# First four tiles as one group of four tokens, with scores by head pair

## The chip, the cores and the metric

The kernel runs on one core of a Trainium2 chip. The metric is the time of one execution in microseconds of device time; smaller is better. A core has five engines that each work through a queue of their own in order: TensorE (PE, matrix products), VectorE (DVE), ScalarE (ACT), GpSimd (POOL) and SyncE (SP, which here issues nearly all DMAs). PEld stands for TensorE's loads of the stationary operand. They meet only through semaphores.

## The reference

Attention over 4 batches, 8 heads, 768 positions and a head size of 64, with a window of 96 positions, 8 global positions at the start and a linear distance penalty, is followed by a feed-forward layer that takes the largest of three products.

```python
scores = q @ k.T / sqrt(64)
rel = pos[:, None] - pos[None, :]
is_global = pos[None, :] < 8
is_local  = (rel >= 0) & (rel < 96)
dist   = where(is_global & ~is_local, 96, abs(rel))
scores = scores - slope[h] * dist          # slope[h] = 2 ** -(h + 1)
scores = where(is_global | is_local, scores, -1e9)
a   = softmax(scores)
x   = (a @ v), heads side by side          # 3072 tokens x 512
h   = max(x @ w1, x @ w2, x @ w3)          # 512 x 768 each
out = h @ w_out                            # 768 x 512
```

## The kernel before, in words

A tile is 128 tokens; there are 24 tiles, six to a batch, and t is the tile's place in its batch. Everything is computed in bf16 with fp32 sums in PSUM. Since the window is 96 long, a tile of queries needs the keys of its own tile and of the one before it; the 8 global positions are put in place of the first 8 keys of the earlier tile, which no query of the window reaches (`put_kg`, `put_vg`; letters G and V).

The order of the work is written out in the string `SCHEDULE`. Each word is a unit: a letter, then the tile or chunk, then a choice of engine where there is one (0 ACT, 1 DVE, 2 POOL, and for transposes 4 stands for a DMA transpose on SP). Each engine's queue is the order in which the units name that engine. The units that matter here:

- `l`, `c`, `x`: load, cast to bf16 and transpose (PE, then a copy out of PSUM) of q and k for a group of tiles, listed in `GROUPS`. A group of n tiles gives each partition n neighbouring tokens, so one descriptor of the load reads n x 256 bytes, and the copy out of PSUM puts tokens back in their order. Before, tiles 0 to 11 come in groups of 2, 2, 2, 4 and 2.
- `L`, `C`, `X`: the same for single tiles 12 to 23; `v` loads a tile of v, and `C` with a 1 in its second place casts it.
- `K`: one exponential per head on ACT that makes the multiplicative mask `wmask` (line 300). `B`: one product per head that makes the additive mask `bias` (line 295).
- `S`: scores of one tile for four heads (two matmuls of 64 rows at a time, line 283), and one exponential out of PSUM on ACT into P (line 288). Where its last number is 1, a matmul of `bias` by the identity (line 275) puts the mask into PSUM ahead of the scores.
- `M`: the product of P and `wmask` on DVE (lines 307 and 309), left out where `bias` was used.
- `A`: 8 or 16 matmuls of P by v with a column of ones (lines 322 and 325), then on DVE the reciprocal of the sum and the product that gives `xb` (lines 331 and 332).
- `T`: transposes `xb` into `xT`, by PE and a copy (lines 349 and 350), or by DMA (line 340).
- `w`, `W`, `o`, `Q`: load and cast of the feed-forward weights. w1 to w3 come in two pieces each: columns 0 to 255 and the 512 columns behind them.
- `F c.f.j`: the product of chunk c with the 128 columns f of weight j, four matmuls (line 361). j = 0 is copied out of PSUM by ACT (line 366); j = 1 and 2 are taken into the running maximum by DVE (lines 368 and 370). A chunk is 4, 2, 2, 4, 4, 4 or 4 tiles (`sizes`). Three PSUM buffers (`psH`) serve all of them.
- `O`: the output product of one tile, six matmuls of 512 columns (line 376), a copy (line 382) and the store. `E`: the last chunk's outputs. `D`: dummy matmuls of zeros.

The string is a fixed order, so what an engine waits for is decided by it alone, and not by the order in which data arrive.

Of the kernel before, what the change touches and what calls it, by code (L numbers as in the profile page):

```python
# [25 lines left out]
    K0 K1 K2 K3 K4 K5 l1.0 l1.1 D0.3 c0.0.2 B0.1 B1.1 B2.1 B3.0 K6 B4.1 B5.1 c0.1.1 c1.0.2 x0.0.4 B6.1  # L26
    B7.1 x0.1.4 S0.0.1 v0 l2.0 l2.1 K7 S0.1.1 G0.0 S1.0.1 S1.1.0 x1.0.3 c1.1.2 M0.0 M0.1 M1.0 v1 x1.1.4
    C0.1.2 v2 A0.1 G1.2 S2.0.1 M1.1 c2.0.2 x2.0.1 C1.1.1 S2.1.0 G2.2 S3.0.1 M2.0 M2.1 C2.1.1 T0.1 S3.1.1
    M3.0 M3.1 c2.1.2 v3 A1.0 C3.1.0 w0.0 V1.2 x2.1.2 w1.0 A2.1 V2.2 A3.0 T1.0 T2.1 T3.1 W1.0.1 W0.0.0
    G3.2 S4.0.0 S4.1.0 F0.0.0 F0.1.0 M4.0 F0.2.0 F0.3.0 G4.1 S5.0.0 M4.1 S5.1.0 w0.1 W0.1.1 w0.2 W0.2.2  # L30
    V3.2 F0.0.1 F0.1.1 F0.0.2 F0.1.2 v4 C4.1.0 A4.0 V4.2 w1.1 W1.1.2 W2.0.0 F0.4.0 F0.5.0 M5.0 M5.1 w1.2
    W1.2.2 v5 W2.1.0 T4.0 F0.2.1 F0.3.1 l3.0 l3.2 F0.4.1 l3.1 c3.0.2 c3.2.2 F0.5.1 o2 C5.1.0 A5.1 l3.3
    F0.2.2 Q2.2 F0.3.2 W2.2.0 o0 T5.0 F0.4.2 o1 F0.5.2 x3.0.0 F1.0.0 F1.1.0 c3.1.1 F1.2.0 x3.2.0 Q0.2
    F1.0.1 F1.1.1 F1.2.1 l4.0 l4.1 c3.3.0 F1.0.2 F1.1.2 F1.2.2 x3.1.2 x3.3.1 F1.3.0 F1.4.0 Q1.2 F1.3.1
    S6.0.0 S6.1.0 v6 v7 v8 G6.0 F1.3.2 F1.5.0 v9 c4.0.1 F1.4.1 S7.0.0 S7.1.0 G7.2 v10 M6.0 M6.1 M7.0
    M7.1 O0.0.0 F1.4.2 c4.1.1 C6.1.2 C7.1.2 L12 F1.5.1 S8.0.0 S8.1.0 x4.0.0 O0.1.0 A6.0 x4.1.2 A7.1 V7.2
    F1.5.2 v11 T6.0 O0.2.0 T7.1 G8.2 C8.1.2 S9.0.0 S9.1.0 G9.1 v12 v13 O0.3.0 F2.0.0 F2.1.0 S10.0.0 M8.0
    M8.1 M9.0 M9.1 S10.1.0 C9.1.2 L13 L14 F2.0.1 F2.1.1 F2.0.2 A8.0 C12.0.1 F2.1.2 G10.2 O1.0.0 V8.2
    A9.1 X12.1 M10.0 M10.1 C10.1.0 C11.1.0 F2.2.0 S11.0.0 S11.1.0 M11.0 M11.1 L15 F2.3.0 F2.4.0 O1.1.0
    V9.2 A10.1 F2.2.1 V10.2 T8.0 F2.3.1 F2.5.0 T9.0 A11.1 F2.4.1 T10.0 F2.2.2 F2.3.2 T11.1 F2.4.2  # L40
    S12.0.0 S12.1.0 F2.5.1 C13.0.2 C14.0.2 C15.0.1 X13.4 F3.0.0 F3.1.0 F3.0.1 G12.1 C12.1.0 F3.2.0
    F3.1.1 F3.2.1 S13.0.0 S13.1.0 F2.5.2 v14 C13.1.0 C14.1.2 M12.0 M12.1 F3.0.2 F3.1.2 X14.4 F3.2.2
    X15.4 G13.2 M13.0 M13.1 S14.0.0 S14.1.0 F3.3.0 F3.4.0 F3.5.0 M14.0 M14.1 G14.1 A12.0 A13.1 F3.3.1
    F3.4.1 F3.5.1 S15.0.0 M15.0 S15.1.0 G15.0 v15 V13.2 L16 L17 v16 T12.4 v17 M15.1 O2.0.0 C15.1.0 A14.0
    V14.2 F3.3.2 F3.4.2 T13.4 F3.5.2 C16.1.0 C16.0.2 X16.3 T14.4 C17.0.2 A15.1 X17.4 O2.1.0 S16.0.0
    S16.1.0 G16.1 L18 V15.2 L19 T15.1 M16.0 O3.0.0 M16.1 F4.0.0 F4.1.0 F4.0.1 F4.1.1 C18.0.2 L20 C19.0.2
    A16.1 F4.2.0 F4.3.0 S17.0.0 S17.1.0 F4.2.1 F4.0.2 F4.3.1 v18 M17.0 v19 M17.1 X18.3 X19.4 C20.0.0
    V16.2 F4.1.2 C17.1.2 O3.1.1 A17.1 F4.2.2 F4.3.2 S18.0.0 M18.0 S18.1.0 M18.1 F4.4.0 T16.4 T17.4
    F4.4.1 C18.1.2 C19.1.1 F4.4.2 X20.4 G18.1 S19.0.0 S19.1.0 F4.5.0 L21 M19.0 M19.1 v20 F4.5.1 A18.0
    T18.4 F4.5.2 A19.1 T19.4 V19.1 C21.0.1 X21.4 G19.1 L22 C22.0.2 L23 X22.4 O3.2.1 O3.3.0 O4.0.1  # L50
    S20.0.0 S20.1.0 M20.0 G20.0 O4.1.0 F5.0.0 F5.1.0 F5.2.0 S21.0.0 S21.1.0 G21.2 F5.0.1 F5.1.1 M20.1
    M21.0 F5.3.0 F5.0.2 F5.1.2 F5.2.1 F5.2.2 v21 C20.1.1 C21.1.2 F5.4.0 S22.0.0 M21.1 S22.1.0 C23.0.0
    F5.3.1 M22.0 M22.1 F5.5.0 F5.3.2 A20.0 V20.2 G22.2 v22 F5.4.1 X23.4 v23 F5.5.1 T20.4 A21.1 V21.1
    T21.4 F5.4.2 F5.5.2 S23.0.0 S23.1.0 M23.0 O4.2.0 M23.1 C22.1.2 A22.0 C23.1.0 O4.3.0 V22.2 T22.4
    A23.1 T23.4 O5.0.1 O5.1.0 O5.2.1 O5.3.0 F6.0.0 F6.1.0 F6.0.1 F6.0.2 F6.2.0 F6.3.0 F6.4.0 F6.1.1
    F6.2.1 F6.1.2 F6.3.1 F6.4.1 F6.2.2 F6.3.2 F6.5.0 F6.4.2 F6.5.1 F6.5.2 E
# [4 lines left out]
def kernel(  # L61
# [27 lines left out]
    sizes = [4, 2, 2, 4, 4, 4, 4]  # L89

    GROUPS = [[0, 2], [2, 2], [4, 2], [6, 4], [10, 2]]
# [8 lines left out]
    NSTART = sizes[0]  # L100
# [21 lines left out]
    zeros = persist.tile([128, 512], BF16, name="zeros")  # L122
# [3 lines left out]
    bias = persist.tile([128, 2, 2, 2, 3, 128], BF16, name="bias")  # L126
    NVA = 4
    va_ring = [persist.tile([128, H * 65], BF16, name=f"va{i}") for i in range(NVA)]
    va_first = [persist.tile([128, H * 65], BF16, name=f"vaf{i}") for i in range(2)]
    kg8 = [persist.tile([128, NP, NG], BF16, name=f"kg8_{i}") for i in range(2)]  # L130
# [5 lines left out]
    va, masked = {}, {}  # L136
# [7 lines left out]
    def part(n, s):  # L144

        T0, sz = GROUPS[n]
        jn = {2: 4, 4: 2, 6: 1}[sz]
        a, x = divmod(s, 4 // jn)
        return divmod(T0, NT) + (sz, a, x * jn, jn)

    def load_part(n, s):

        bb, t0, sz, a, j0, jn = part(n, s)
        r = raw_pool.tile([128, 2 * DM], FP32, name="rawp", tag="raw")
        r = r[:, 0:sz * jn * 128].rearrange("i (h x) -> i h x", h=2 * jn)
        raw["p", n, s] = r
        src = (q, k)[a][bb, 2 * j0:2 * (j0 + jn), t0 * 128:(t0 + sz) * 128, :]
        nc.sync.dma_start(out=r, in_=src.rearrange("h (i e) d -> i h (e d)", e=sz))
# [19 lines left out]
    def cast_part(n, s, how):  # L178
        bb, t0, sz, a, j0, jn = part(n, s)
        qk = cast_pool.tile([128, 2 * DM], BF16, name="qkp", tag="qkb")  # L180
        qk = qk[:, 0:sz * jn * 128].rearrange("i (e h d) -> i e h d", e=sz, d=D)
        qb["p", n, s] = qk
        copies[how](qk, raw["p", n, s].rearrange("i h (e d) -> i e h d", e=sz))  # L183
# [42 lines left out]
    def u_x(n, s, how):  # L226
# [14 lines left out]
        for (lo, hi, pool, tag, copy), tp in zip(halves, tps):  # L241

            copy(dst[:, lo:hi], tp.rearrange("c e j i -> c j i e"))  # L243
# [24 lines left out]
    def u_S(T, g, how):  # L268
# [3 lines left out]
        if how:  # L272

            for hh in range(2):
                nc.tensor.matmul(sp[:, hh, :, 0:n], identb,  # L275
                                 bias[:, g, hh, :, 0:2] if t else bias[:, g, hh, :, 2:3],
                                 start=True, stop=False, skip_group_check=True)
        for ds in range(2 if t else 1):
            for j2 in range(2):
                jp = 2 * g + j2  # L280
                for hh in range(2):
                    hsl = slice(64 * hh, 64 * hh + 64)
                    nc.tensor.matmul(sp[:, hh, j2, ds], qT(T - ds, 1)[hsl, jp], qT(T, 0)[hsl, jp],  # L283
                                     start=not how, stop=True, skip_group_check=True)
        P = p_pool.tile([128, 4, 2, 128], BF16, name="P", tag="P")
        Pt[T, g] = P
        masked[T, g] = how
# [3 lines left out]
    def u_B(h, how):  # L291
        g, hp = divmod(h, 4)
        j2, hh = divmod(hp, 2)
        mul = (nc.scalar.mul, nc.vector.tensor_scalar_mul, nc.gpsimd.tensor_scalar_mul)[how]
        mul(bias[:, g, hh, j2], rbase, -slopes[h] / scale)
# [6 lines left out]
    def u_M(T, g):  # L302
        P = Pt[T, g]
        if masked[T, g]:
            return
        if T % NT:
            nc.vector.tensor_mul(P, P, wmask[:, g, :, 0:2])  # L307
        else:
            nc.vector.tensor_mul(P[:, :, 0], P[:, :, 0], wmask[:, g, :, 2])

    def u_A(T, how):

        b, t = divmod(T, NT)
        op = psS.tile([128, 2, 512], FP32, name="op", tag=f"sp{how}")
        for g in range(2):
            P = Pt[T, g]
            for j2 in range(2):
                for hh in range(2):
                    h = 4 * g + 2 * j2 + hh
                    i = 2 * hh + j2  # L320
# [189 lines left out]
```

The softmax here doesn't subtract the row's maximum and nothing guards it: scores larger than these inputs give would overflow.

## Time and profile before

| What | Value |
|---|---|
| median of 3 runs | 180.32 us (180.25 to 180.33) |
| span of the profiled execution | 178.5 us |
| what lies around that span, from the median | 1.8 us |
| granted TensorE clock, mean | 0.997 |
| PE busy | 167.1 us (94% of the span) |
| DVE, ACT, POOL busy | 119.1, 103.2, 37.4 us |
| first feed-forward matmul | 23.3 us |

The page gives no other time for the profiled execution than its span; the median of the runs is measured without the profiler's cut at the first and last instruction, and the difference is taken as constant. A row of the groups gives line, engine, operation, names and shapes, how often, then busy time, mean length of one in ns, and the engine's idle time just before such instructions with what ended it. Matmuls overlap, so the cost of one is read from the chain, where a stretch of so many matmuls has a length, and not from its mean length.

### The profile page before, as it was taken

What the parts mean: (1) busy time and instruction counts of PE and PEld (TensorE: products, weight loads), DVE (VectorE), ACT (ScalarE), POOL (GpSimd) and SP (SyncE); (2) the same over time, 40 slices, a digit from 0 to 9 for tenths busy, and PEclk for the clock granted to TensorE, in tenths of its full rate; (3) what the DMA queues carried; (4) which work ended last, traced back from release to release, by engine and by line L of the source; (5) the groups of instructions that cost most, each with busy time, mean ns of one, the idle gap of its engine ahead of it and who ended that gap; (6) DMA issues with size and microseconds to landing.
All of it is one profiled execution on the core that took longest, in us unless ns stands there. A gap on an engine that the chain in (4) does not pass through costs nothing.

```text
span 178.5 us, 3963 instructions
## 1 busy us (share of the span) xinstructions
PE 167.1 (94%) x1529; PEld 95.9 (54%) x1551; DVE 119.1 (67%) x237; ACT 103.2 (58%) x160; POOL 37.4 (21%) x65
## 2 busy tenths in 40 slices
PE   3599799999999999999999999999999999999991
PEld 0455645458866677845555555454454555444451
DVE  4519975977796689748978448978358986137610
ACT  4867898646689958555753936351862543440131
POOL 4255203543343012210006024100020401000000
PEclk9999999999999999999999999999999999999998
DMA  5999999999998899899544999988989664700015
GB/s 139 292 270 243 357 321 383 319 361 356 252 194 229 218 254 227 142 204 234 92 90 122 167 253 231 145 172 152 182 156 300 123 129 147 252 12 4 0 47 190
DMA packets 83587, 35.52 MB, mean 199 GB/s; under 512 B 66160, under 2 KB 78320, under 8 KB 83568
## 3 DMA queue, kind: packets, MB, share of 16 engines
q1 hardware_dynamic: 83424, 35.20, 83.6%
q8 instruction: 12, 0.20, 0.5%
q10 hardware_dynamic: 144, 0.07, 0.1%
q14 instruction: 7, 0.06, 0.1%
HBM read 25.17 MB, written 6.29 MB: 176 GB/s over the span
## 4 chain that ended last, share of the span: by engine, by line
PE 88%; ACT 3%; DVE 2%; POOL 2%; issue 1%; DMA 1%; POOLq 0%; ACTq 0%
PE h L361 53%; PE po L376 16%; PE sp L283 7%; PE op L322 3%; PE op L325 3%; PE tpp L239 3%; PE xtp L349 2%; ACT wmask L300 2%; PE sp L275 2%; DMA out_dram<-ost 1%; DVE qkT L243 1%; DVE xb L332 1%; ACT ost L382 1%; ACT P L288 1%; PE tp L261 1%
## 5 line engine op out<-in xcount | busy, mean ns | idle before, releaser
L361 PE MATMUL h<-xT,w 128*128 128x512 bf16 (+1 forms) x491 | 99.2, 348 | 0.7 <-issue 0.2
L361 PEld LDWEIGHTS <-w 128*128 128x128 bf16 x504 | 47.0, 98 | 40.4 <-ACT w L427 0.2
L288 ACT ACTIVATE P<-sp 128x1024 bf16<-128x1024 f32 (+1 forms) x48 | 43.4, 954 | 20.4 <-PE sp L283 20.2
L368 DVE TENSOR_TENSOR h<-h,h 128x512 bf16<-128x512 bf16 (+1 forms) x42 | 25.2, 609 | 25.6 <-PE h L361 15.5
L366 ACT CAST h<-h 128x512 bf16<-128x512 f32 (+1 forms) x42 | 21.6, 532 | 21.5 <-PE h L361 21.3
L376 PE MATMUL po<-wo,ht 128*128 128x512 bf16 (+2 forms) x147 | 33.1, 362 | 0.5
L370 DVE TENSOR_TENSOR ht<-h,h 128x512 bf16<-128x512 bf16 (+1 forms) x42 | 25.0, 606 | 3.7 <-PE h L361 3.0
L307 DVE TENSOR_TENSOR P<-P,wmask 128x1024 bf16<-128x1024 bf16 x36 | 24.8, 716 | 3.6 <-ACT P L288 3.5
L382 ACT COPY ost<-po 128x512 f32<-128x512 f32 (+2 forms) x20 | 11.2, 564 | 18.4 <-PE po L376 11.2
L376 PEld LDWEIGHTS <-ht 128*128 128x128 bf16 x156 | 14.0, 98 | 13.8
L332 DVE TENSOR_TENSOR xb<-op,rz 128x512 bf16<-128x512 f32 x24 | 16.6, 691 | 0.8
L283 PEld LDWEIGHTS <-qkT 64*128 64x128 bf16 x352 | 10.2, 96 | 10.0 <-issue 8.0
L283 PE MATMUL sp<-qkT 64*128 64x128 bf16 x352 | 15.2, 223 | 0.4 <-DVE xb L332 0.4
L322 PEld LDWEIGHTS <-P 128*128 128x128 bf16 x192 | 12.5, 97 | 2.7 <-ACT P L288 0.2
L221 POOL COPY va<-vaf 8x260 int32<-8x260 int32 x14 | 6.3, 449 | 34.7 <-PE op L325 34.7
L198 POOL CAST qkb<-raw 128x1024 bf16<-128x1024 f32 x7 | 7.2, 1037 | 27.6 <-DMA raw<-in_k_dram 27.6
L322 PE MATMUL op<-va,P 128*128 128x65 bf16 x160 | 12.4, 193 | 0.3 <-ACT va L189 0.2
L239 PE MATMUL tpp<-identb,qkp 128*128 128x128 bf16 x96 | 8.5, 246 | 4.0 <-POOL qkp L183 3.5
L325 PEld LDWEIGHTS <-P 128*128 128x128 bf16 x160 | 10.4, 97 | 1.8 <-issue 0.2
L239 PEld LDWEIGHTS <-qkp 128*128 128x128 bf16 x96 | 7.0, 112 | 5.8 <-POOL qkp L183 4.4
L325 PE MATMUL op<-va,P 128*128 128x65 bf16 x128 | 9.9, 193 | 0.1
L243 ACT COPY qkT<-tpp 128x1024 bf16<-128x1024 bf16 (+1 forms) x9 | 7.9, 873 | 3.4 <-PE tpp L239 3.4
(66 smaller groups left out, 107.7 us busy)
## 6 DMA issues: line engine op xcount, KB each, us to landing
rawv<-in_v_dram SPq DMA_DIRECT2D x24, 256.0 KB, 4.9
out_dram<-ost SPq DMA_DIRECT2D x23, 256.0 KB, 2.3
rawp<-in_q_dram SPq DMA_DIRECT2D x6, 512.0 KB, 7.3
rawp<-in_k_dram SPq DMA_DIRECT2D x6, 512.0 KB, 7.7
wst<-in_moe_w_dram SPq DMA_DIRECT2D x3, 1024.0 KB, 10.3
raw<-in_q_dram SPq DMA_DIRECT2D x12, 256.0 KB, 4.2
raw<-in_k_dram SPq DMA_DIRECT2D x12, 256.0 KB, 4.7
wst<-in_moe_w_dram SPq DMA_DIRECT2D x3, 512.0 KB, 8.6
```

Source lines behind the costliest of these rows:

```text
L239: nc.tensor.transpose(tp[:, e, j - lo], qb["p", n, s][:, e, 2 * j:2 * j + 2].rearrange("i h d -> i (h d)"), identb)
L283: nc.tensor.matmul(sp[:, hh, j2, ds], qT(T - ds, 1)[hsl, jp], qT(T, 0)[hsl, jp], start=not how, stop=True, skip_group_check=True)
L288: nc.scalar.activation(P[:, :, 0:n], sp.rearrange("p a b d n -> p (a b) d n")[:, :, 0:n], AF.Exp, bias=0.0, scale=scale)
L307: nc.vector.tensor_mul(P, P, wmask[:, g, :, 0:2])
L322: nc.tensor.matmul(o, P[:, i, 0], heads(va[T])[:, h], start=True, stop=(t == 0), skip_group_check=True)
L325: nc.tensor.matmul(o, P[:, i, 1], heads(va[T - 1])[:, h], start=False, stop=True, skip_group_check=True)
L332: nc.vector.tensor_tensor(out=x.rearrange("p (g h) d -> p g h d", g=2), in0=o4[:, :, :, 0:64], in1=rz[:, :, :, None].to_broadcast([128, 2, ...
L361: nc.tensor.matmul(ps, w123[f // 2][:, dm, j, (f % 2) * 128:(f % 2) * 128 + 128], xT[c][:, dm], start=(dm == 0), stop=(dm == 3))
L366: nc.scalar.copy(h01, ps)
L368: nc.vector.tensor_max(h01s[c, f], h01s[c, f], ps)
L370: nc.vector.tensor_max(ht[c][:, f], h01s[c, f], ps)
L376: nc.tensor.matmul(po, ht[c][:, f, tt * 128:(tt + 1) * 128], wo[:, f, cols], start=(f == 0), stop=(f == NF - 1))
```

## The change

The first four tiles become one group of four tokens in a partition, in eight pieces: q and k by head pair (64 x 2 columns). Queries of these tiles are copied out of PSUM as they stand, by token within the group and then by partition (`u_x`, for n = 0 and a = 0), and keys are put in order as before.

New units: `s tp.jp` computes the scores of one head pair for two tiles (tp = 0: tiles 0 and 1; tp = 1: tiles 2 and 3). The queries are read as four blocks of 32 columns. The exponential reads PSUM in the order of tokens and writes P in natural order, in two instructions of 384 elements for tp = 0 and one of 1024 for tp = 1. `m tp.jp` multiplies such a P by `wmask` on DVE or POOL. `g T.jp` puts the global keys in place of tile 1's first 8 keys (for tile 2's queries), and for tile 3's queries makes a copy `k2x` of tile 2's keys with the global ones in it, since tile 2's own keys are still needed. The three parts of `wmask` stand in another order. The unit `B`, the tensor `bias` and its matmuls are gone. P of tiles 2 and 3 is held in a buffer of the weight staging pool.

Chunks are now 2, 2, 2, 2, 4, 4, 4, 4 tiles, where two neighbours share `xT` and `ht`. `A` with a 2 uses two `psH` buffers and normalises in two halves. `load_w` can load in two halves. The dummy matmuls have 128 columns, and the order is a new one: tiles 8, 12 to 23 have `xb` transposed by DMA (before: 12, 13, 14, 16 to 23), and tiles 13 to 23 have q and k transposed by DMA (before: 13, 14, 15, 17, 19 to 23).

```diff
-    sizes = [4, 2, 2, 4, 4, 4, 4]
-    GROUPS = [[0, 2], [2, 2], [4, 2], [6, 4], [10, 2]]
+    sizes = [2, 2, 2, 2, 4, 4, 4, 4]
+    GROUPS = [[0, 4], [4, 2], [6, 4], [10, 2]]
...
+    BIG = [0, 0, 1, 1, 2, 3, 4, 5]
...
-        jn = {2: 4, 4: 2, 6: 1}[sz]
+        jn = 1 if n == 0 else {2: 4, 4: 2, 6: 1}[sz]
...
+            if n == 0 and a == 0:
+                copy(batch_T(0)[:, 0, j0 + lo:j0 + hi, 0:sz * 128].rearrange("c j (e i) -> c j e i", e=sz),
+                     tp.rearrange("c e j i -> c j e i"))
+            else:
+                copy(dst[:, lo:hi], tp.rearrange("c e j i -> c j i e"))
...
-        if how:
-
-            for hh in range(2):
-                nc.tensor.matmul(sp[:, hh, :, 0:n], identb,
-                                 bias[:, g, hh, :, 0:2] if t else bias[:, g, hh, :, 2:3],
-                                 start=True, stop=False, skip_group_check=True)
...
-        mul(bias[:, g, hh, j2], rbase, -slopes[h] / scale)
+    def u_g(T, jp, how):
+
+        k0 = qT(0, 1)[:, jp, 0:NG]
+        if T == 1:
+            copies[how](qT(1, 1)[:, jp, 0:NG], k0)
+        else:
+            copies[how](k2x[:, jp, NG:128], qT(2, 1)[:, jp, NG:128])
+            copies[how](k2x[:, jp, 0:NG], k0)
+
+    def u_s(tp, jp, how):
+
+        sp = psS.tile([128, 2, 4, 128], FP32, name="sp", tag=f"sp{how}")
+        g, j2 = divmod(jp, 2)
+        tiles = (2 * tp, 2 * tp + 1)
+        lo = 0 if tp else 1
+        for i, T in enumerate(tiles):
+            for ds in range(2 if T else 1):
+                for hh in range(2):
+                    hsl = slice(64 * hh, 64 * hh + 64)
+                    qs = qkT[0][hsl, 0, jp, 0:512].rearrange("c (e i) -> c e i", e=4)[:, :, 32 * T:32 * T + 32]
+                    ks = k2x[hsl, jp] if T - ds == 2 and ds else qT(T - ds, 1)[hsl, jp]
+                    nc.tensor.matmul(sp[:, hh, 2 * i + ds if T else 1], ks, qs,
+                                     start=True, stop=True, skip_group_check=True)
+        if tp:
+            if "P1" not in Pt:
+                Pt["P1"] = stage_pool.tile([128, 4, 2, 4, 128], BF16, name="P1", tag="wst1")
+            P = Pt["P1"][:, jp]
+        else:
+            P = p_pool.tile([128, 2, 4, 128], BF16, name="P0", tag="P")
+        Pt["s", tp, jp] = P
+        for hh in range(1 + lo):
+            o, x = (P[:, hh, 1:4], sp[:, hh, 1:4]) if lo else (P.rearrange("p h b n -> p (h b) n"),
+                                                               sp.rearrange("p h b n -> p (h b) n"))
+            nc.scalar.activation(o.rearrange("p b (i e) -> p b i e", e=4), x.rearrange("p b (e i) -> p b i e", e=4),
+                                 AF.Exp, bias=0.0, scale=scale)
+
+    def u_m(tp, jp, how):
+        g, j2 = divmod(jp, 2)
+        P = Pt["s", tp, jp]
+        mul = (nc.vector, nc.gpsimd)[how].tensor_mul
+        if tp:
+            wm = wmask[:, g, j2::2, 1:3].rearrange("p a s n -> p a (s n)")[:, :, None].to_broadcast([128, 2, 2, 256])
+            Pv = P.rearrange("p h (i s) n -> p h i (s n)", i=2)
+            mul(Pv, Pv, wm)
+        else:
+            mul(P[:, :, 1:4], P[:, :, 1:4], wmask[:, g, j2::2])
...
+        if how == 2:
+            ops = [psH.tile([128, 512], FP32, name="op", tag="h") for _ in range(2)]
```

The new order up to the first blocks of the feed-forward layer's second weight column:

```diff
+    K0 l0.6 K4 K2 c0.6.2 x0.6.1 K3 K5 l0.0 c0.0.2 x0.0.3 l0.4 c0.4.2 K1 x0.4.4 l0.2 c0.2.1 x0.2.3 l0.1
+    g2.0.1 K7 s0.0.1 c0.1.2 s0.2.0 l0.5 c0.5.1 x0.5.4 l0.3 l0.7 c0.7.1 x0.1.3 c0.3.2 g2.2.1 K6 g1.2.2
+    g1.0.2 g2.1.1 x0.3.2 x0.7.3 s0.1.1 s0.3.0 g1.1.2 s1.0.1 m0.2.0 s1.2.0 w0.0.0 g1.3.1 g2.3.1 s1.3.1 v0
+    C0.1.1 m0.3.0 m0.1.0 m0.0.0 A0.2 m1.0.0 s1.1.0 v1 C1.1.2 m1.3.0 W0.0.0 A1.1 m1.1.0 m1.2.1 D5.6 T0.0
+    V1.2 T1.1 v2 C2.1.2 A2.2 V2.0 F0.0.0 v3 C3.1.2 G0.0 A3.1 V3.0 w1.0.0 W2.0.2 w0.1.0 T2.0 F0.4.0
+    F0.1.0 T3.0 F0.5.0 W1.0.1 W0.1.2 F0.1.1 w0.2.0 W0.2.2 l1.0 c1.0.2 G3.0 F1.0.0 F1.0.1 F1.1.0 F1.1.1
+    F1.2.0 F0.1.2 F0.2.0 l1.1 c1.1.1 x1.0.2 F0.0.1 F0.0.2 x1.1.4 F1.1.2 F1.4.0 S4.0 S4.1 G4.2 F1.0.2
```

## The prediction, made before the changed kernel ran

> **What bounds the kernel now.** I read the page's slices first, then busy time by stage, what TensorE (PE) waited for, the chain of waits, and the groups by form for prices. The slices (4.46 us each) show an idle PE only at the start and in the last slice:
>
> ```profile
> PE   3599799999999999999999999999999999999991
> ```
>
> Cut into stages at the joints of the chain, per stage length, PE busy, weight load, DVE, ACT and POOL busy:
>
> ```profile
> 3.76:9.50 5.74, 2.84 (x23) 2.06 (x24) 3.88 (x10) 4.47 (x11) 1.84 (x2) 1.00 1.21 297
> 9.50:13.45 3.95, 3.95 (x37) 2.32 (x37) 0.19 (x1) 3.18 (x6) 2.06 (x4) 1.00 1.24 269
> 13.45:18.50 5.05, 4.67 (x67) 2.61 (x66) 5.02 (x8) 3.81 (x5) 2.24 (x3) 1.00 1.28 244
> 18.50:23.30 4.80, 3.84 (x85) 3.22 (x85) 4.11 (x11) 4.20 (x6) 0.94 (x3) 1.00 1.07 370
> 23.30:172.10 148.80, 147.59 (x1302) 83.63 (x1322) 104.18 (x195) 83.80 (x129) 28.14 (x42) 1.00 0.82 190
> ```
>
> From 23.30 to 172.10 PE is busy 147.59 of 148.80 us, and all that its waits hold after 23.3 is one line:
>
> ```profile
> PE h L361 <- issue: 0.2, 1, 0.2
> ```
>
> So the time is three terms: the start of the first feed-forward matmul (23.30), the PE work that is left then (148.8), and a tail of 6.4 us that the change leaves as it is. The chain (start, length, what) shows what sets the first, and PE's prices:
>
> ```profile
> 7.69 1.01 PE tpp L239 x8
> ...
> 21.61 0.70 DVE xb L332
> 22.31 0.05 issue
> 22.35 0.40 PE xtp L349 x4
> 22.75 0.55 PE sp L283 x16
> 23.30 0.34 PE h L361
> ...
> 41.04 0.45 PE tpp L239 x8
> ...
> 43.24 2.62 PE h L361 x24
> ...
> 154.09 7.55 PE h L361 x35
> ```
>
> Tile 3's normalised output (xb, DVE) is the last link ahead of the dense stretch. A 256-column matmul costs 2.62/24 = 0.109 us, a 512-column one 7.55/35 = 0.216, a transpose 0.45/8 = 0.056, sixteen score matmuls 0.55. Early on, a transpose took 1.01/8 = 0.126. Prices for DVE and ACT, by form:
>
> ```profile
> L288 ACT ACTIVATE P<-sp 128x1024 bf16<-128x1024 f32 x40 | 39.0, 1027 | 15.3 <-PE sp L283 15.1
> L307 DVE TENSOR_TENSOR P<-P,wmask 128x1024 bf16<-128x1024 bf16 x36 | 24.8, 716 | 3.6 <-ACT P L288 3.5
> ...
> L300 ACT ACTIVATE wmask<-rbase 128x384 bf16<-128x384 f32 x8 | 3.6, 509 | 1.5 <-DVE rbase L470 1.5
> ```
>
> **What the Trainium skill says.** "TensorE: Matmul & The Clock Gate", Part 1: the array runs at half rate until a free-running window of some 3.4 us was busy. The trace agrees: transposes start 107 ns apart until 13.45 us and 56 ns apart afterwards; the stretch of 3.4 us before was 89% streaming by my count of starts, the one before that 69%. "GPSIMD Engine Reference", section 3.1: a two-input operation of 2048 fp32 takes 4497 ns; before has none on POOL, so I estimate 2.2 us for 1024. "SBUF — State Buffer", Who interferes with whom: a DVE operation with two SBUF inputs contends with a POOL read. Agreed: L307 has a median of 686 ns and a maximum of 1095, at 139.9 us, beside a POOL cast of 0.88 instead of 0.61. "DMA: Bandwidth & Descriptors", Specifications, gives line rate from 512 B. Here 512-byte pieces moved at 290 GB/s (2.5 to 9 us) and mostly 1-KB pieces at 362 (36 to 40 us); the measurement decides.
>
> **The change part by part.**
>
> *PE work.* Twelve bias matmuls (L275) go: four of 256 and eight of 512 columns, 2.2 us warm, all ahead of 23.3, so their worth lies only in the start. Splitting the first chunk of four tiles makes 144 matmuls of 256 from 72 of 512: 15.72 − 15.53 = +0.19 us. Two tiles of q/k (16 and 18) and two of attention output (8 and 15) move from PE transposes to DMA: 16 × 0.056 + 8 × 0.056 = −1.34 us. Each needs about 3.3 us (q/k) or 2.4 us (output) to land. In the new order at least 3.9 us of PE work separates an output from its first use (tile 23, the tightest; needed: 1.1 for DVE + 2.4). For q/k (X17 to X19) the order leaves as little as 0 us between unit and use, but SP runs ahead of PE: counted from its cast I find 2 to 3 us to spare. Bound: 0 to 1 us of waits. The four added transposes hold SP for 1.24 us each, 5 us in all; SP waited 29.6 us for output copies alone, so loads queued behind them have room.
>
> *The start.* DMA: the first group now comes as eight pieces of 256 KB in 1-KB runs. Packets begin at 2.6 us; 2.1 MB at 357 GB/s is 5.9 us, and data were used some 0.7 us after their bytes: the last piece is usable at 9.2, where before its 2 MB needed until 10.5. Weights w0.0 then come ahead of v, w1.0 straight after it, and tiles 4 and 5 after the first weights: w0.0 lands near 11, v1 13.4, w1.0 18.7, w0.2 21.7 us (256-byte pieces at 205 GB/s, 2-KB at 375), before about 22 to 27. None of this bounds the first block.
>
> ACT: eight wmask exponentials (0.43 a step), three copies of 0.58, eight exponentials of 384 (0.41 a step) and four of 1024 (0.97 a step; a pair took 1.94) are 3.5 + 1.7 + 3.3 + 3.9 = 12.4 us from 3.76, plus about 0.8 idle ahead of the first k: they end at 16.9. Before, tile 3's last one ended at 19.5. Reading PSUM out of order I cost at nothing: the ACT copy of qkT, which permutes too, took 580 ns for 512 elements, the unpermuted xT copy 587. If it doubled the 12 exponentials, ACT would be 7 us late; nothing shows that.
>
> DVE becomes the bound, since the masks of tiles 0 to 3 that the bias replaced come back: four of 768 (about 0.55) and three of 1024 (0.69); the seven bias products (0.35 each) go, long covered. From 13.05, when the fourth pair's exponential ends: three masks 1.45, tile 0's normalisation in two halves 1.4, two masks 1.25 (+0.3 for POOL's multiply beside them), tile 1's 0.9, one mask 0.6, xT 0.35, tile 2's 1.4. Sum 7.65, so xb of tile 2 is there at 20.7 and tile 3's at 21.6. PE then transposes tile 2 (20.9) and goes on with feed-forward blocks of tiles 0 and 1, which it no longer leaves. With the array cold, A1, A2, A3 and the first block take twice as long: tile 2 goes in at 21.8. I take 21.4. POOL's multiply has from 15.1 until A2 needs what is queued behind it, V1 and the cast of v2 (1.1 us): up to 3.3 us it costs nothing; at 6 it would cost 2.7.
>
> The small copies that replace the one keys copy per tile (nine on DVE of about 0.17 each, as the kg copies took, three on POOL of 0.22) fall before 13, where DVE still waits for the last k and v; without that cover they would add 1.5. The probabilities of tiles 2 and 3 live in a weight staging buffer, so the third large weight load (w1.2) waits until A3 is done, near 21; in SP's order its turn comes after 30 anyway, it lands near 35, and the first block that needs it stands near 38: nothing.
>
> *Work left at 21.4.* Against before at 23.30: the scores of tile 4 (+0.55), 16 transposes of tiles 4 and 5 (+0.89) and two tiles' xT (+0.44) are still to do, one 256-block is done (−0.44); with the −1.34 and +0.19 above, +0.29. About eight pairs of score blocks are torn apart; eight score matmuls alone took 0.33 instead of half of 0.55: +0.4. A 256-block gives its PSUM buffer 0.9 us to be emptied where a 512-block gave 1.7, and an exponential of 1.0 on ACT stands between: two waits of 0.2 around S4 and S5, taken as 0.4 (bounds 0 to 1.5; before lost nothing, on fewer such blocks).
>
> *Sum.* 21.4 − 23.3 = −1.9; +0.29 + 0.4 + 0.4 = +1.1; net −0.8. The profiled span is 178.5; the median 180.32 stands 1.8 above it, for what lies around. 180.3 − 0.8 = 179.5.
>
> **The rivals.** *Cold array (slower).* The bias matmuls were what kept PE streaming between 8.5 and 12; in their place are score blocks with gaps, 55 to 70% of the time by my count. If the clock is still at half rate when the dense stretch begins, that begins at 21.8 and half of up to 3.4 us is lost: 21.8 + 1.7 + 1.1 − 23.3 = +1.3, 181.6; typical 181.0. It decides from about 1.6 us of dense work at half rate. For it: 69% did not warm the array before. Against: six dummy matmuls, and from 16 us on PE is nearly full if cold, so that a window ends busy by about 21. *Nothing gained.* The start is earlier, but 256-blocks wait for PSUM buffers in four chunks instead of two, or late DMA transposes take it back: 1.9 us earlier, 1.9 given back, 180.3. For it: the thinner cover; against: 256-blocks ran at 0.109 without a wait before. *More gained.* The array is warm early and DVE steps overlap as they did: start 20.9, no waits: −2.4 + 0.29 + 0.4 = −1.7, 178.6.
>
> **How the numbers follow.** A measurement of this kernel tells 0.2% (0.36 us) from no change. Forecast 50% (0.45 faster, 0.05 same), more gained 12% (faster), nothing gained 15% (0.10 same, 0.05 slower), cold array or a wait of its size 23% (0.22 slower, 0.01 same): faster 0.57, same 0.16, slower 0.27. The forecast's own range is 178.9 to 180.1. Cases of both signs hold much, so the range reaches from 178.0 (more gained, and the DMA work earlier still) to 181.6.
>
> **What would show it.** Right: tile 2's xtp near 21 us, h blocks dense behind it, PE waits after that under 1 us, tpp at 56 ns a start before 20. Wrong: L342 on POOL above 3.3 us; exponentials of 384 well above 0.51; 256-blocks at 0.21 instead of 0.109 past 22 (cold); waits of h for ACT or DVE, or of sp for a DMA, adding up to over 1.5 us; a first dense block later than 23.3.

## The result, and the profile after

The changed kernel takes **185.44 us** (median of 4 runs, 184.44 to 186.99), the kernel before 180.32: a ratio of 1.029 (95% interval 1.024 to 1.034). It is slower, outside the range of the forecast. The profiled execution has a span of 184.0 us (before 178.5), and its run took 185.79. Medians and ranges, here and below, are of all executions; ratios, and what is said of spreads, leave out those more than 1.5% above the fastest of their kernel.

The slices of PE, 4.6 us each, as shown of before:

```profile
PE   0688599999999999999999999999999999999991
```

The thin place is now the fifth slice, 18.4 to 23 us. Stages cut at this kernel's own joints, with the columns of before (stage, length, PE busy, weight load, DVE, ACT, POOL; then the granted clock, the DMA share and GB/s):

```profile
13.45:18.50 5.05, 4.08 (x60) 3.18 (x56) 4.37 (x10) 4.60 (x6) 3.41 (x3) 1.00 1.10 297
18.50:22.50 4.00, 1.81 (x26) 1.55 (x24) 3.81 (x6) 1.04 (x2) 2.83 (x5) 1.00 1.11 341
22.50:26.70 4.20, 4.20 (x40) 3.45 (x38) 2.44 (x6) 2.37 (x7) 2.94 (x3) 1.00 1.15 322
26.70:177.60 150.90, 149.63 (x1392) 89.30 (x1391) 108.74 (x208) 83.38 (x137) 29.84 (x42) 1.00 0.86 184
177.60:184.00 6.40, 2.71 (x25) 1.75 (x23) 0.29 (x1) 2.25 (x5) 0.00 (x0) 0.98 0.46 164
```

The tail is 6.4 us, as before. From 18.5 to 22.5 us PE does 1.81 us of work while DVE is busy for 3.81 of 4.00: DVE sets the start. The chain of waits (start, length, what) says with what:

```profile
13.83 1.92 DVE P L344 x3
...
17.42 2.88 DVE P L342 x2
...
20.45 0.70 DVE xb L396
...
21.20 0.61 PE xtp L415 x4
...
24.42 0.43 PE xtp L415 x4
24.85 1.71 PE h L428 x8
```

Two mask products of 1024 (L342) take 2.88 us in the chain (2.96 in the timeline, to the end of the second) where the forecast had 1.25 + 0.3. Then tile 2's transposes come at 24.2 us, not 21.4, and the eight feed-forward matmuls of 256 columns behind them take 1.71/8 = 0.214 us each: twice the warm price of 0.109. The step to full rate is at 26.75 us; behind it 36 take 3.93. (The clock column reads 1.00 in all these rows; half rate shows only in the spacing.)

The two timelines, DVE and then POOL, put names to it:

```profile
17.34 2.96 DVE L342 TENSOR_TENSOR P<-P,wmask 128x1024 bf16<-128x1024 bf16 x2
```

```profile
15.71 2.12 POOL L342 TENSOR_TENSOR P<-P,wmask 128x1024 bf16<-128x1024 bf16 x1 [0.39 <-ACT P L332]
18.02 0.62 POOL L232 COPY va<-vaf 8x260 int32<-8x260 int32 x1 [0.18 <-POOL P L342]
18.59 1.16 POOL L200 CAST va<-rawv 128x512 bf16<-128x512 f32 x2
```

POOL's own product ran for 2.12 us, and nearly all the time that DVE's two ran POOL had something of its own: the end of that product, a copy, two casts. The first of the two, beside the end of POOL's product, took 1.05 us, the second, beside the copy and the casts, 1.99. PE's waits, of which 2.2 us at one place is tile 1's `xb` (`h01s` is the running maximum of a feed-forward block):

```profile
PE xtp L415 <- DVE xb L396: 2.2, 1, 2.2
...
PE h L428 <- DVE h01s L439: 0.5, 2, 0.3
```

**The balance.** To size the waits behind the start I took from each gap between two matmul starts the price of the first one (0.216, 0.109, 0.056, 0.028 for a score, 0.030 for an attention matmul) and added up what is left. In the trace of before 22 matmul records are missing; each is counted at 0.216.

| term | forecast | measured | miss |
|---|---|---|---|
| tile 2's transposes (start) | 21.4 us | 24.23 us | +2.8 |
| dense work at half rate behind it | none | 1.2 us | +1.2 |
| PE work left, against before at 23.3 | +0.29 us | +0.2 us | −0.1 |
| torn score blocks and waits beyond those of before | +0.8 us | 7.35 − 4.25 = +3.1 us | +2.3 |

The misses add up to 6.2; the span is 184.0 for a forecast of 178.5 − 0.8 = 177.7, which is 6.3. Three things are to be explained: the start, the half rate and the waits.

Not all that this count holds is waiting. Between a block of score matmuls (64 rows) and any other matmul PE loses the same time in every trace here, 0.096 us on the way in and 0.120 on the way out. Before has 19 such blocks behind its start, 4.1 of its 4.25 us, and, missing records apart, no other gap above 0.04. The changed kernel has 22, which is 4.75, and nine other gaps of 0.08 to 0.45 us, 2.4 together. Ahead of the first two, at 37.3 and 38.4 us, DVE and then POOL had this:

```profile
34.98 2.28 DVE L360 TENSOR_TENSOR P<-P,wmask 128x1024 bf16<-128x1024 bf16 x2
```

```profile
34.23 2.48 POOL L503 CAST w<-wst 128x1024 bf16<-128x1024 f32 x2
```

### The profile page after: what moved, and what is told of

Its sections match the earlier page's. It is cut to its first block, busy times and chain, and to the rows that moved or that the text cites. A ratio compares the mean times of both kernels' runs of the same rounds, so it can differ in the third digit from the quotient of the medians.

```text
span 184.0 us, 4101 instructions
## 1 busy us (share of the span) xinstructions
PE 169.2 (92%) x1590; PEld 103.6 (56%) x1590; DVE 126.1 (69%) x261; ACT 103.1 (56%) x174; POOL 44.7 (24%) x70
## 4 chain that ended last, share of the span: by engine, by line
PE 78%; DVE 10%; DMA 4%; ACT 4%; issue 2%; SPq 1%; ACTq 0%
PE h L428 46%; PE po L448 15%; PE sp L292 5%; PE tpp L250 3%; PE op L377 3%; DMA rawp<-in_q_dram 3%; DVE P L360 3%; PE op L380 3%; ACT P L296 2%; PE xtp L415 2%; DVE P L342 2%; DMA out_dram<-ost 1%; DVE P L362 1%; DVE P L344 1%; ACT P L332 1%
## 5 line engine op out<-in xcount | busy, mean ns | idle before, releaser
L428 PE MATMUL h<-xT,w 128*128 128x256 bf16 (+1 forms) x576 | 103.5, 329 | 0.7 <-DVE h01s L439 0.5
L428 PEld LDWEIGHTS <-w 128*128 128x128 bf16 x576 | 54.3, 99 | 36.2 <-issue 1.2
L296 ACT ACTIVATE P<-sp 128x1024 bf16<-128x1024 f32 (+1 forms) x40 | 36.5, 961 | 16.1 <-PE sp L292 16.1
L437 ACT CAST h<-h 128x512 bf16<-128x512 f32 x24 | 14.1, 587 | 20.7 <-PE h L428 20.5
L439 DVE TENSOR_TENSOR h<-h,h 128x512 bf16<-128x512 bf16 x24 | 16.4, 685 | 11.6 <-PE h L428 11.4
L200 POOL CAST va<-rawv 128x512 bf16<-128x512 f32 x16 | 11.5, 730 | 36.2 <-DMA rawv<-in_v_dram 28.7
L441 DVE TENSOR_TENSOR ht<-h,h 128x512 bf16<-128x512 bf16 x24 | 16.1, 684 | 4.1 <-PE h L428 3.3
L439 DVE TENSOR_TENSOR h01s<-h01s,h 128x256 bf16<-128x256 bf16 x24 | 9.6, 416 | 6.3 <-PE h L428 2.7
L437 ACT CAST h01s<-h 128x256 bf16<-128x256 f32 x24 | 8.9, 374 | 6.7 <-PE h L428 5.3
L292 PE MATMUL sp<-qkT 64*128 64x128 bf16 x296 | 12.1, 218 | 0.3 <-DVE xb L396 0.3
```

Of the source, the lines that this page charges most:

```text
L296: nc.scalar.activation(P[:, :, 0:n], sp.rearrange("p a b d n -> p (a b) d n")[:, :, 0:n], AF.Exp, bias=0.0, scale=scale)
L428: nc.tensor.matmul(ps, w123[f // 2][:, dm, j, (f % 2) * 128:(f % 2) * 128 + 128], xT[B][:, dm, o], start=(dm == 0), stop=(dm == 3))
L437: nc.scalar.copy(h01, ps)
L439: nc.vector.tensor_max(h01, h01, ps)
L441: nc.vector.tensor_max(ht[B][:, f, o], h01, ps)
```

## Experiments on the start

Each group ran on one chip with the kernel before, which stood at 180.4 to 180.5 us in all of them and within 0.6 us from run to run but for one run of 182.4. The changed kernels spread more, by up to 2.7 us, so the profiled execution and the ratio's interval weigh more here than a difference of 1 us between two medians.

**The mask product on POOL.**

```diff
-m1.1.0 m1.2.1 D5.6
+m1.1.0 m1.2.0 D5.6
```

> The changed kernel with one word altered: the mask product of tiles 2 and 3 for the third head pair runs on DVE instead of POOL. Theory P (POOL's two-input product blocked DVE's two mask products beside it, which took 2.96 us together in the changed kernel instead of 1.3, and so made tile 1's output late): tile 1's transposes begin about 1.5 us earlier (near 19.7 instead of 21.2), DVE gets 0.6 of work more behind that, and PE has no gap of 2.5 us any more in which its clock window fails; together 1.5 to 3 us faster than the changed kernel, 182.5 to 184. Theory C (the half-rate array alone sets the start): within 0.5 us of 185.4, since the product only moved.

184.1 us (182.37 to 185.31), ratio 1.016 [1.012, 1.020]. DVE's timeline:

```profile
17.70 1.28 DVE L342 TENSOR_TENSOR P<-P,wmask 128x1024 bf16<-128x1024 bf16 x2
...
19.74 2.60 DVE L342 TENSOR_TENSOR P<-P,wmask 128x1024 bf16<-128x1024 bf16 x2
```

The first pair takes 1.28 us, and tile 1's transposes come at 19.88 instead of 21.20. But the second pair now runs beside POOL's casts of v and takes 2.60, so tile 2's come at 24.56: the cost has moved from one pair to the other.

**An array warmed by dummies, early only.**

```diff
-c0.6.2 x0.6.1 ... c0.0.2 x0.0.3 l0.4 c0.4.2 K1 x0.4.4 l0.2 c0.2.1 x0.2.3
+c0.6.2 D0.28 x0.6.1 ... c0.0.2 D0.3 x0.0.3 l0.4 c0.4.2 K1 D0.9 x0.4.4 l0.2 c0.2.1 D0.4 x0.2.3
```

> The changed kernel with 44 more dummy matmuls of 128 columns, placed where PE waited before 8 us (28 ahead of the first transposes, 3, 9 and 4 ahead of the next ones). They leave nothing out and cost PE only time in which it waited. Theory C (without the bias matmuls the array stays at half rate until 26.75 us, and that is what the change lost): transposes and score matmuls step at 56 ns and 28 ns from about 8 us on, the first 256-blocks at 0.109 instead of 0.213, and the time falls by 2.0 to 3.0 us, to about 183. Theory P: PE waits for DVE's mask products all the same, tile 1's transposes stay near 21, and only what ran at half rate from 21.6 to 26.75 is saved, half of about 4.2 us; so both give a gain here, P 1.5 to 2.1 at the most.

> Both edits: the mask product on DVE, and the 44 dummy matmuls. If the two losses are separate terms, the gains of the two runs add up: 3.5 to 5 us, 180.5 to 182, with tile 2's transposes near 21.5 as predicted for the change and a steady 0.109 per 256-column matmul from there. If they are one loss seen twice (the late DVE leaves PE idle, and the idle window keeps the clock at half rate), the sum is smaller than the two gains together by 1 us or more. What then still lies above 179.5 is neither: the splitting into 256-blocks, torn score blocks and mask products beside POOL casts after 30 us.

Dummies alone: 184.48 us (184.11 to 184.84), ratio 1.023 [1.021, 1.024]. With the mask on DVE as well: 183.02 (181.75 to 186.48), 1.012 [1.009, 1.014]. The granted clock of the first kernel, in tenths by slices of 4.56 us (it reads full before its first step):

```profile
PEclk9975879999999999999999999999999999999999
```

By the steps of this clock the array was at full rate from 4.8 us, at half from 11.7, at full from 18.5 and at half again from 21.9 to 25.3. So dummies alone left the first blocks at half rate, with tile 2 at 24.21, and the edit did not do what it was for. The second fall follows a wait of 2.6 us for tile 1's `xb`: there a late DVE is seen to cost the clock. In the second kernel, at half rate from 12.7 to 22.9, tile 2 came at 23.03 us.

**Warm all through.** As the last one, with more dummies behind most of the scores, 0.06 us each, up to the first feed-forward block (D0.26 before `x0.4.4`, D0.6 before `s0.0.1`, D0.12 behind `s0.2.0`, and so on).

> The changed kernel with every mask product on DVE and dummy matmuls in all of PE's waits from 1 to 22 us, so that no window is left thin. Theory 'half rate and the mask beside POOL explain the start': transposes 56 ns apart from about 8 us on without a relapse, tile 2's xtp at 21.5 to 22.3 us, no 256-column matmul at 0.21, and 181.0 to 182.0 us with a spread under 1 us; what then stays above my 179.5 is waits after 27 us. Theory 'PE's rate early does not matter, DVE sets the start': as with both earlier edits, 183 us, tile 2's xtp at 23. If dummies delay real work by their PSUM buffers: later than 23.5.

184.81 us (183.8 to 186.99), ratio 1.024 [1.022, 1.025]; profiled span 182.0. The array is warm from 5.8 us on and stays so, and no 256-column matmul shows 0.21. Tile 2's transposes nevertheless come at 23.13. DVE's timeline, then POOL's:

```profile
16.85 2.59 DVE L342 TENSOR_TENSOR P<-P,wmask 128x1024 bf16<-128x1024 bf16 x2
...
20.20 1.49 DVE L342 TENSOR_TENSOR P<-P,wmask 128x1024 bf16<-128x1024 bf16 x2
```

```profile
16.96 0.82 POOL L232 COPY va<-vaf 8x260 int32<-8x260 int32 x1 [1.67 <-issue]
17.74 1.16 POOL L200 CAST va<-rawv 128x512 bf16<-128x512 f32 x2
```

A faster PE only brought the products forward into POOL's other work. With PE at full rate DVE still sets the start.

**POOL's work given to ACT.** The same warm kernel, and the one without dummies, with the first-rows copy of v1, two v casts and one weight cast on ACT:

```diff
-V1.2 ... C2.1.2 ... C3.1.2 ... W2.0.2
+V1.0 ... C2.1.0 ... C3.1.0 ... W2.0.0
```

> The kernel with every mask product on DVE and dummies in all of PE's waits (array warm from 7 us), and with five POOL operations of 16 to 24 us given to ACT, which idles there: the first-rows copy of v1, the casts of v2 and v3, and one weight cast. Theory 'any POOL work beside a DVE product of two inputs slows it': the four 1024 products drop from 2.59 + 1.49 us to about 2.8 in all, tile 1's xb comes at 19.2 instead of 20.2 and tile 2's xtp at 21.8 to 22.1 instead of 23.13; about 1.2 us less in span than the 182.0 of its parent. Theory 'DVE's products are slow for another reason (permuted operand, PSUM traffic)': they stay at 1.2 us each, and the time too.

> The changed kernel with every mask product on DVE and the same POOL operations given to ACT, but no dummies: the array as cold as in the changed kernel. With contention gone and the clock left: tile 1's xtp at about 19.1 us, tile 2's at 22.5 to 23.5 at half rate, time 182 to 183 us with a spread of 2 us or more. If the clock is worth nothing because DVE sets the start, it equals the warm twin to within 0.5 us.

185.43 us (184.99 to 187.2), ratio 1.030 [1.027, 1.033], and 187.13 (184.71 to 188.56), 1.033 [1.029, 1.037]. All four products took 1.28 a pair, as the contention theory wanted, and tile 1's transposes came at 18.98 in the warm one; but I had put v3's cast behind a copy that waits for tile 2's attention, and the weight cast behind that. The feed-forward blocks behind tile 2's transposes waited for that weight: they began at 24.20 (warm), with the transposes done at 22.8. A cost taken away, two new waits made by the edit.

**The start put right.** The weight cast stays on POOL, and both v casts stand ahead of tile 2's attention:

```diff
-V1.2 ... v2 C2.1.2 A2.2 V2.0 F0.0.0 v3 C3.1.2
+V1.0 ... v2 C2.1.0 v3 C3.1.0 A2.2 V2.0 F0.0.0
```

> The warm kernel (every mask product on DVE, dummies in PE's waits) with the first-rows copy of v1 and the casts of v2 and v3 on ACT and both casts ahead of tile 2's attention, while the weight cast stays on POOL. Theory 'masks beside POOL plus half rate plus nothing else made the start late': tile 1's xtp at 19.0 us, tile 2's at 21.5 to 21.9, feed-forward dense behind it, span 180.3 to 180.8 against 182.0 of the kernel that differs only in these, which is 182.1 to 182.6 us. What it then stands above the forecast's span of 177.7 is waits behind the start. Rival: the start is bound by yet another link (v3's load, ACT), tile 2's xtp after 22.5.

> The same start without the dummies, the array left to its own clock. If half rate is worth what the earlier pair suggested (1 us) or less, since DVE sets the start: 182.5 to 183.5 us, tile 2's xtp at 22 to 22.5, with a wider spread than the warm twin. If the clock is worth 2 us or more alone: 184 us or more.

Warm: 183.01 us (182.18 to 183.06), ratio 1.012 [1.008, 1.016], profiled span 180.4. Without dummies: 183.1 (181.62 to 185.92), ratio 1.012 [1.008, 1.016], span 180.9. DVE's timeline of the warm one, then PE's:

```profile
16.87 1.28 DVE L342 TENSOR_TENSOR P<-P,wmask 128x1024 bf16<-128x1024 bf16 x2
...
18.92 1.28 DVE L342 TENSOR_TENSOR P<-P,wmask 128x1024 bf16<-128x1024 bf16 x2
```

```profile
21.64 0.39 PE L415 MATMUL xtp<-identb,xb 128*128 128x128 bf16 x4
22.21 1.05 PE L428 MATMUL h<-xT,w 128*128 128x256 bf16 x8 [0.19 <-POOL w L503]
```

This is the forecast's start: 21.64 for 21.4. Against the warm kernel that differs only in where those copies run, and in v3's load, which comes earlier with its cast (23.13), POOL beside DVE was worth 1.5 us. Left to its own clock the start is 22.30, so half rate on the way was worth 0.7 in that execution, in which the array was at full rate again from 19.2 us, before the dense blocks began. And still the time is 1.2% above before: the rest is behind the start, where the count above gives 7.55 us for the warm one and 4.25 for before.

**What the bias matmuls had done.** The kernel before without them (S0.0.1 to S0.0.0 and so on; the six mask products that they had saved are back on DVE, and the products that made `bias` are gone), and again with dummy matmuls of as many columns in their place:

```diff
-S0.0.1 ... S0.1.1 ... S1.0.1 ... S2.0.1 ... S3.0.1 ... S3.1.1
+D0.1 S0.0.0 ... D0.1 S0.1.0 ... D0.2 S1.0.0 ... D0.2 S2.0.0 ... D0.2 S3.0.0 ... D0.2 S3.1.0
```

> The kernel before, with the bias matmuls and bias products left out and the mask products on DVE in their place for tiles 0 to 3; the rest of its order as it was. Theory C: without the twelve long matmuls PE streams less between 8.5 and 12 us, the clock step at 13.45 us comes one or more windows later (16.9 or after), while the time changes by what DVE adds: six mask products, 2 of 0.42 and 4 of 0.69, 3.6 us, of which perhaps half lies on the way to tile 3's output. So 1.5 to 4 us slower than before. Rival (the bias matmuls had no part in the clock): the clock step stays within 0.5 us of 13.45.

> The kernel before without its bias matmuls (masks of tiles 0 to 3 multiplied on DVE), but with dummy matmuls of the same count of columns where each bias matmul stood, so PE streams as before while DVE keeps the seven added mask products. Theory 'clock': what the bias matmuls bought was mainly an array that stays in stream, so the clock steps up near 13.5 us again and the time comes back from 185.9 to 181 to 182 us, with a narrow spread. Theory 'masks': the seven products of 0.55 to 0.69 us on DVE are what cost, the first dense block stays near 25.7 us and the time at 183 us or more even with a warm array. Both shares: about 182.5.

185.88 us (183.51 to 186.26), ratio 1.028 [1.023, 1.032]; with the dummies 184.39 (183.47 to 186.81), 1.021 [1.018, 1.025], three of six runs at 183.5. Taking out the bias matmuls alone costs the old order as much as the whole change. In the profiled run without dummies the clock step is at 18.9 us (before 13.5) and the first dense block at 25.7, 2.4 later than before, with DVE's products and normalisations one behind the other in the chain; dummies kept the clock step at 13.5 but not the block (26.4 in the profile, where the array is at half rate again from 23.7 to 27.1). The best runs of the two are equal, 3.1 us behind before. So most of what the bias matmuls bought appears to be a DVE without mask products, and the rest, in some runs, the clock.

## Experiments on the waits

**Blocks of 256.** The kernel before, each unit of the first chunk in two halves:

```diff
+        if c == 0 and half is None:
+            u_F1(c, f, j, 0)
+            u_F1(c, f, j, 1)
+            return
...
+            W, o = 256, slice(256 * half, 256 * half + 256)
```

> The kernel before with its first chunk of four tiles computed as two blocks of 256 columns instead of one of 512 in every feed-forward unit, order unchanged: the change's block size alone. By my sum +0.19 us of PE work and at most 0.4 us of waits for PSUM buffers: 180.5 to 181.1 us. Rival: blocks of 256 with exponentials and mask products of 1 us between them on ACT and DVE make PE wait, which would be the 2 us of waits past 27 us that the changed kernel shows: 182 to 183 us.

182.44 us (182.36 to 182.66), ratio 1.012 [1.010, 1.013], span +2.2. My sum had +0.19 of work and up to 0.4 of waits. The waits by my count grow from 4.25 to 6.13. PE's waits, and the chain ahead of the first:

```profile
PE h L368 <- ACT h01s L377: 0.7, 1, 0.7
...
PE h L368 <- DVE h01s L379: 0.6, 1, 0.6
```

```profile
22.36 0.94 ACT w L438
...
24.29 1.02 ACT P L288
25.31 0.27 ACT h01s L377
...
25.63 1.47 PE h L368 x12
```

A block of 256 fills its `psH` buffer in 0.44 us; three buffers cover 1.3 us of queue. On ACT a weight cast and two exponentials (1.94 together) stand ahead of the copy that frees the first buffer; on DVE two mask products of tile 5 stand ahead of the maxima, 2.58 us because POOL casts weights beside them (2.48 us at 33.06). With blocks of 512 three buffers cover 2.6 us. Two attempts to take one of these waits away:

```diff
-S4.0.0 S4.1.0 F0.0.0 F0.1.0 M4.0
+S4.0.0 F0.0.0 F0.1.0 S4.1.0 M4.0
```

> The kernel before with its first chunk in blocks of 256 columns, as in the earlier run at 182.44 us, but with the second score unit of tile 4 moved behind the first two feed-forward units. There PE waited 0.72 us for ACT, whose queue held a weight cast and two exponentials of 1 us ahead of the first copy of a block. Theory 'the blocks wait because the copies stand behind exponentials in ACT's order': the wait at 25 us falls to 0.2 us or less, 181.6 to 181.9 us; the 0.6 us wait for DVE at 36 us (mask products of 2.58 us beside a POOL cast) stays. Theory '256-blocks lose in another way': no change, 182.4 us.

```diff
-F0.4.0 F0.5.0 M5.0 M5.1 w1.2 W1.2.2 v5 W2.1.0 T4.0 F0.2.1 F0.3.1
+F0.4.0 F0.5.0 w1.2 W1.2.2 v5 W2.1.0 T4.0 F0.2.1 F0.3.1 M5.0 M5.1
```

> The kernel before with its first chunk in blocks of 256 columns and tile 5's two mask products moved behind two more feed-forward units, so that they run on DVE after POOL's weight casts instead of beside them (they took 2.58 us there, 1.3 alone). Theory 'PE's wait of 0.6 us at 36 us comes from mask products beside POOL ahead of the maxima': that wait goes, the products take about 1.4 us, 181.7 to 182.0 us for the 182.44 of the kernel without the move. Rival: any DVE product of 1.3 us ahead of the maxima makes 256-blocks wait: unchanged within 0.2.

Scores torn apart: 182.34 us (181.92 to 182.41), ratio 1.010 [1.009, 1.011]. The gap for ACT fell from 0.88 to 0.13 us, as the theory said, but the count still comes to 5.89 and the time is the same: one more block of scores costs 0.22, and a gap of 0.3 for a DMA transpose has come at 155.5 us. Masks later: 183.52 (183.31 to 184.31), 1.017 [1.013, 1.021]; the wait for DVE did not go, it grew:

```profile
PE h L368 <- DVE h01s L379: 1.6, 1, 1.6
```

The two products now ran beside another POOL cast, took 2.10 us instead of the 1.4 that was meant, and stood ahead of other maxima; what a move clear of POOL's casts is worth was not tested. What holds is plainer: with 1.3 us of cover, two exponentials (1.94) or two products beside POOL (2.1 to 2.6) ahead of a copy make PE wait. That no order avoids this was not shown.

**The DMA transposes.** The kernel before with four transposes moved from PE to DMA, with the two of q and k alone, and with these and the order mended (`X16.4` behind `T14.4`, S16 behind two feed-forward units):

```diff
-T8.0 ... A14.0 ... C16.0.2 X16.3 ... T15.1 ... X18.3
+T8.4 ... C16.0.2 X16.4 A14.0 ... T15.4 ... X18.4
```

> The kernel before with tiles 16 and 18 (q/k) and 8 and 15 (attention output) transposed by DMA instead of PE, nothing else: the step that I sized at -1.34 us of PE work with 0 to 1 us of waits. If that holds: 179.0 to 179.6 us (180.4 - 1.34 + up to 0.5). Rival: the transposes land late or hold back SP's queue, so that PE waits as long as it saved: 180.2 to 181.5 us, with a wait of sp or h for a DMA in the trace.

> The kernel before with only tiles 16 and 18 of q/k transposed by DMA (16 PE transposes fewer, 0.89 us), the attention output left on PE. In the earlier run with four such moves PE waited 8.6 us for tile 15's transpose, which stood in SP's order behind loads that waited for buffers. If only that one was misplaced: 179.4 to 180.0 us. If DMA transposes as such hold SP or land late here: 180.4 us or more, with a wait of sp for a DMA.

> The kernel before with tiles 16 and 18 of q/k transposed by DMA, tile 16's transpose now behind tile 14's attention transpose in SP's order, and tile 16's scores moved behind the last output of chunk 3 and two feed-forward units, so that 4 us of PE work cover it. Theory 'a DMA transpose saves its PE time if SP's order and the cover are right': 179.4 to 179.9 us (180.4 - 0.89 + up to 0.4), no wait of h or sp for a DMA above 0.3 us. Rival: DMA transposes displace something else again: 180.4 us or more.

191.13 us (1.059 [1.057, 1.062]), 181.71 (1.007 [1.006, 1.008]), 181.87 (1.007 [1.006, 1.009]): never faster. PE's waits name the reason, one line from each of the three in this order:

```profile
PE h L361 <- DMA xT<-xb: 9.3, 2, 8.6
```

```profile
PE h L361 <- DMA xT<-xb: 1.5, 1, 1.5
```

```profile
PE sp L282 <- DMA qkT<-qkb: 1.3, 1, 1.3
```

In the first, tile 15's transpose stood in SP's order behind the loads of tiles 18 and 19 and was issued only at 104.6 us, and behind that wait the array ran at half rate until 113 us; in the second tile 16's (1.28 us of SP) held up two attention transposes; in the third, room made for those left tile 16's own late. The first of these was my misplacement. The second and third show that in this order 16 PE transposes (0.89 us) cost less than what replaced them.

**Tile 23 in the changed order.** In the clean warm kernel the largest single wait was 1.0 us at 154.6 us, for tile 23's transpose by DMA. It goes back to PE:

```diff
-A23.1 T23.4
+A23.1 T23.0
```

> The warm kernel with the clean start, and tile 23's attention output transposed by PE (4 transposes, 0.22 us, and an ACT copy of 0.58) instead of DMA. Theory 'the wait at 154.6 us is for that DMA transpose alone': the 1.0 us gap shrinks to at most 0.3 us, span 179.7 to 180.0 us against 180.4, the median 0.4 to 0.7 us below the 183.0 of the kernel without the edit. Rival: the block then waits for the ACT copy or something else of the same size: no change within 0.2 us.

183.84 us (183.18 to 184.74), ratio 1.019 [1.017, 1.022]: not faster. PE now waits for DVE itself, once at the start and once (1.1 us) at tile 23, and in this execution for the transpose of tile 21's q and k by DMA, of which the clean kernel's profile had nothing:

```profile
PE xtp L415 <- DVE xb L396: 2.1, 2, 1.1
PE sp L292 <- DMA qkT<-qkb: 1.2, 1, 1.2
```

The rival held: one wait took the other's place. The second line shows a wait that some executions have and some have not.

## Why the prediction was wrong

- **The bound and the form of the sum were right.** Start, work left and tail are the three terms; the tail is 6.4 us, the work left +0.2 for +0.29.
- **The step that failed first is DVE's sum from 13.05 us.** "Two masks 1.25 (+0.3 for POOL's multiply beside them)" measured 2.96, and the three masks ahead of them 1.91 for 1.45 (the third, beside a POOL cast, 0.96); the sum also began at 13.83 (13.35 in the warm kernel). "Up to 3.3 us it costs nothing" asked only who waits for POOL's result; POOL's product was done in 2.12 (estimate 2.2), yet cost DVE while it ran. The +0.3 was about right for that product alone (1.05 for 0.68); left out were the copy and the casts queued behind it, which made the second product 1.99. The Trainium skill's page "SBUF — State Buffer", Who interferes with whom, says that a DVE operation with two SBUF inputs and a POOL read share a pair of ports which one of them holds alone, and that the order of issue decides which of them blocks; the trace agrees: one product took 1.99 us, 0.68 without POOL beside it. I had priced it by the maximum in the trace of before (1095 ns, beside a single cast). With POOL away from them and the array warm the sum holds: 21.64 for 21.4.
- **The cold array was seen as a rival, at 23%, and came.** Its clock step was at 26.75 us, not by 21. The sum gave it +1.3 net; measured it cost 1.2 of dense work, and 0.7 of start where DVE left room for it. What it had wrong was to stand alone: PE was thin from 18.5 to 22.5 (1.81 of 4.00) because DVE was late, so the array did not warm; with early dummies, too, the clock fell behind just such a wait. Two cases I had kept apart are one.
- **The waits were sized at a quarter.** "A 256-block gives its PSUM buffer 0.9 us" was right in kind, "two waits of 0.2" and bounds "0 to 1.5" were not: with the torn blocks I took 0.8; they are 3.1. Three more blocks of scores, one of them tile 4's own, are 0.65 of it: the +0.4 for torn blocks came about by luck, as two blocks more at 0.22 each and not eight pairs at 0.05. The nine gaps are 2.4. Three of them, 1.0 in all, are blocks of 256 that wait for DVE's maxima (1.9 in the old order), and a fourth (0.3) is for a mask product itself. In DVE's queue ahead of these four stand products that ran beside POOL's weight casts: two of 1024 took 2.28 us, as shown, and one of 512, at 51.5 us, 1.27 for 0.42. So the term that failed the start seems to return here. The other five, 1.1 in all, are for `xb`, POOL's cast of v, a copy of ACT and others below 0.15; none ends with a DMA.
- **The DMA term** counted 1.34 us of PE work as a gain and "0 to 1" for waits. In the old order no version of the two q/k moves paid. In the changed kernel's profile the outputs took 3.5 us to land (2.4 used), yet PE waited for none of them behind the start, so the work was gained there; in other profiles of the new order PE waited up to 1.4 us for such transposes.
- **Right, as the trace shows:** the exponentials read PSUM out of order at next to no cost, 492 ns for 384 elements (0.51 used) and 1040 for 1024 (1027 in the natural order):

```profile
L332 ACT ACTIVATE P<-sp 128x1024 bf16<-128x1024 f32 x4 | 3.9, 1040 | 0.5 <-PE sp L320 0.5
...
L332 ACT ACTIVATE P<-sp 128x384 bf16<-128x384 f32 x8 | 3.4, 492 | 0.5 <-PE sp L320 0.4
```

**Open.** Why executions of one kernel differ by up to 2.7 us here. The Trainium skill's page "TensorE: Matmul & The Clock Gate", Part 1, has a free-running window, so a start at the edge of warming could fall either way: the four profiled kernels with the new order and no early dummies, whose PE order is the same, step to full rate first at 26.7, 25.4, 19.9 and 12.4 us. But kernels that were warm throughout in their profiles spread by 0.9 to 2.2 us as well, so this is not the whole reason. That POOL's casts lie behind the waits past the start is read from the trace and not tested: no run took those casts away from DVE's products. No version here beats the kernel before.

## What to carry to other kernels

Where DVE is in the chain, price its two-input products together with everything that POOL does in those microseconds, the small copies too; a product moved to POOL is not off DVE. Before halving a block, divide the longest thing that can stand ahead of its copy in ACT's or DVE's order by the time in which a block fills its PSUM buffer: that many buffers are needed (an estimate: 1.94/0.44 gives five here, and more buffers were not tried). And a matmul that looks redundant may be the one that keeps a product off a busy engine: take it out alone first, which here would have told the sign.

## What the hardware showed that I had not expected

- The array fell back to half rate with no idle stretch above 0.9 us: with early dummies it was at full rate from 4.8 us and at half from 11.7, after 3.4 us in which PE streamed about a third of the time by my count of starts.
- A single DVE product of 1024 bf16 took from 682 to 1992 ns in one kernel, by what POOL did beside it.
- The kernel before ran within 0.6 us nearly always; kernels with the new order spread by 0.7 to 2.7 us, with the same instructions in the same order.
- A block of score matmuls of 64 rows costs PE 0.096 us on the way in and 0.120 on the way out, the same in all 19 traces: tearing one block in two costs 0.22 us.
